# Head 0 loaded straight into its slots, head 1's row maxima placed behind the first scores, and two PSUM banks for turning x where attention ends

## The chip, the cores and the metric

The kernel runs on one core of one Trainium2 chip. The metric is device time of one execution in microseconds (us); less is better. Before the change the median of three runs is 960.9 us (960.69 to 964.77).

## What is computed

Block-sparse attention in float32 over 4 batches of 8 heads, 768 positions and 64 features, then a feed-forward block with a tanh shrink. Cut to what matters:

```python
scores = q @ k.transpose(0, 1, 3, 2) / np.sqrt(64)
mask = window | first and last block | 3 sampled blocks a row   # blocks of 32
scores = np.where(mask, scores, -1e9)
attn = softmax(scores)                  # row maximum subtracted first
x = (attn @ v) -> (3072, 512)
h = x @ w_in                            # 512 x 2048, weights come as int64 words that hold float64
g = h - np.tanh(h)
out = g @ w_out                         # 2048 x 512
```

## The kernel before

**Attention.** Each float32 operand is split into a high part (rounded to the matmul's float32r) and a low part (the rest), and products are made of both. `load_qk` brings the keys and queries of a pair of heads as one `raw` tile of 128 partitions, 64 for each head. `high` (ScalarE, L245) makes `hm`, `low` (GpSimd, L250) makes `lo`, and `dist` (L257) copies the 64 partitions of one head by DMA into that head's slots of one large tile, `slab`: slots A and B (high parts, with the mask rows below them, filled by `fill`, L283) and slots C and D (high and low parts). Head 0's A and B are written by `direct` on VectorE (L253), out of `hm`.

For each head, `smax` (TensorE, L324) makes approximate scores in six tiles of 128 rows, `maxima` (VectorE, L330 for two tiles, L334 for one) takes their row maxima, `turn_max` (TensorE, L337) turns them, `neg_max` (VectorE, L341) negates them, and `put_max` (DMA, L347) writes them as one more row of slot B. Only then can `scores` (TensorE, L356 and L357) make the exact scores with the maximum subtracted inside the product. The work goes in 96 steps, three for each head, and each step has two halves: `scores` into the PSUM tile `pst`, `expo` (ScalarE, L360), `p_high` (ScalarE, L366), `p_low` (GpSimd, L371), and two steps later `accum` (TensorE, L385 to L389) multiplies with v. `smax` has one PSUM tile, `psm`.

**Feed-forward.** Tokens are in six blocks of 512 (n = 0 to 5), the 2048 hidden features in 16 tiles (ft). One unit is one (n, ft): `h_part` (TensorE, L703, 12 matmuls into one of two banks), eleven element operations on ScalarE, VectorE and GpSimd (`g_part`, L713 to L733; VectorE's five are L717, L719, L725, L727 and L729), and `second` (L738 to L740, 12 matmuls into the banks pf0 to pf3). Blocks 0 to 3 are begun during attention with a few ft. Where attention ends, `plan_rest` goes on with the list `SEGS` of (n, first ft, last ft): x=0 is (3, 2, 6), x=1 is (4, 0, 6), x=2 is (5, 0, 16), x=3 is (4, 6, 16). Blocks 4 and 5 must first be turned there: `x_turn` (TensorE, L681, four transposes into bank pf4), `x_high` (ScalarE, L685), `x_low` (VectorE, L689). The weights of ft 6 to 15 are converted there too, 20 of them: three operations on VectorE (L600, L604, L608, through bank pf5 into a buffer `ob`), then ScalarE (L786) and GpSimd (L788). `out_bank` (L797, L799, L801) empties pf0 to pf3 at the end of a segment. For x=1 it writes to the same `ob` buffers, `out_put` (L806) sends them to DRAM, and `get_part` (L758) brings them back into `spare` for x=3.

**The order.** Every step is entered into a `Plan` with a due number, an engine, a duration, and what it reads and writes. `Plan.order` plays the engines against each other and picks on each engine, among the steps that could start within a window `WIN` of the earliest, the one with the smallest due number; the order that comes out is fixed for every engine. DMAs are all issued from SyncE's queue (SP), which is in order too: an issue that waits for a buffer holds up those behind it.

Of the kernel before, what the change touches and what calls it, by code (L numbers as in the profile page):

```python
# [11 lines left out]
F32 = mybir.dt.float32  # L12
# [21 lines left out]
RATE = 1.0  # L34
FT1 = 14
# [9 lines left out]
CHUNK = (28, 52, 68, 84)  # L45

# [24 lines left out]
class Plan:  # L71
# [3 lines left out]
    WIN = {"PE": 0.45, "ACT": 0.3, "DVE": 0.3, "POOL": 0.3, "SP": 0.0}  # L75
# [7 lines left out]
    def order(self):  # L83
# [32 lines left out]
        for _ in range(n):  # L116
            best = None
            for e, c in pools.items():
# [9 lines left out]
                i = min(i for i in c if s[i] <= t0 + self.WIN[e])  # L128
# [87 lines left out]
def attention(ctx, tc, plan, qk, v, samp, blocks, xscr, ident, ffn):  # L216
# [35 lines left out]
    def direct(dst, x):  # L252
        nc.vector.tensor_copy(out=dst[0][0:64], in_=hms[0].bitcast(F32)[0:64, x])  # L253
# [16 lines left out]
    def setup():  # L270
# [6 lines left out]
        nc.vector.tensor_scalar(out=neg[R, :], in0=allow, scalar1=1.0, scalar2=-MASKED, op0=ALU.subtract, op1=ALU.mult)  # L277
        nc.vector.tensor_copy(
# [131 lines left out]
    def at(due, f, *args):  # L410
# [20 lines left out]
        elif n == "direct":  # L431
            eng, dur, r, w, kw = "DVE", dve(768, True), [("hm", 0, args[1])], [("AB"[args[1]], 0)], {"lock": True}
# [6 lines left out]
        elif n == "setup":  # L439
            eng, dur, r, w, kw = "DVE", 1.6, [("st",), ("sp",)], [("mk",)], {"lock": True}  # L440
# [37 lines left out]
        elif n == "p_low":  # L478
            s, x = args
            eng, dur, r, w = "POOL", pool(768), [("pe", s % 2, x), ("ph", s % 3, x)], [("pl", s % 3, x)]  # L480
# [17 lines left out]
    add(-91, "SP", 0.1, lambda: nc.sync.dma_start(out=sp_i[R, :], in_=samp), w=[("sp",)])  # L498
    for x in range(2):
        at(-90 + 0.1 * x, load_qk, 0, x)  # L500
        at(-85 + 0.1 * x, high, 0, x)
        at(-82 + x, direct, (sA, sB)[x], x)
# [4 lines left out]
    at(-86.5, load_qk, 1, slice(0, 2))  # L507
    at(-86, setup)
    at(-84, fill, 0, sA, mk)
    k = -76  # L510
    for c, h in ((CH, 0), (AB, 1), (CL, 0)):
# [18 lines left out]
    k = -63  # L530
# [11 lines left out]
    at(-59, load_v, 0)  # L542
# [16 lines left out]
    for h in range(2, NHEAD):  # L559
# [58 lines left out]
class FFN:  # L618
# [175 lines left out]
    def out_bank(self, x, n, ft, j):  # L794
        nc, o, ob = self.nc, self.banks[j], self.spare[j] if x == 0 else self.ob[j % 2]
# [12 lines left out]
    def turn(self, n, j, x, i):  # L808
        (self.x_turn, self.x_high, self.x_low)[x](n, j, self.xt, *((i,) if x else ()))
# [50 lines left out]
    def unit_ops(self, plan, f, n, ft, h, hq, xi, k, g, gi, halves, **kw):  # L860
# [7 lines left out]
        else:  # L868
            add(f, "PE", 2.72, self.h_part, (n, ft, h, None, xi), rx, [hq], **kw)
# [20 lines left out]
    def plan_rest(self, plan):  # L890
# [104 lines left out]
```

## Time and profile before

| what | value |
|---|---|
| median of 3 runs | 960.9 us |
| the profiled execution's own time | 962.74 us |
| its span, first to last instruction | 961.0 us |
| granted TensorE clock, mean | 0.994 |
| TensorE matmul busy | 903.9 us (94%) |
| VectorE, ScalarE, GpSimd busy | 692.5, 652.3, 531.0 us |
| DMA moved | 123.17 MB |

The span is 1.7 us below the profiled execution's own time, and that execution was 1.8 us above the median. A row of a timeline gives the start and the duration in us, the engine (PE is TensorE, DVE VectorE, ACT ScalarE, POOL GpSimd, SPq the queue that issues DMAs), the source line, what is written and read, and in brackets the idle time ahead of it with what ended it.

### The profile page before, as it was taken

The page shows a single profiled execution, that of the slowest core. Times are in us where ns is not written, and L with a number is a line of the kernel's source. Part 1 is how long each engine was busy: PE and PEld are TensorE (multiplying, and loading weights), DVE is VectorE, ACT ScalarE, POOL GpSimd, SP SyncE. Part 2 cuts the span into 40 slices and gives each one's busy share as a digit, 9 for nine tenths or more (in the row PEclk, how much of TensorE's full clock was granted, in tenths as well). Part 3 has the DMA queues.
Part 4 walks back from the last instruction along what each step waited for, and adds up shares of the span by engine and source line. Part 5 has one row for each costly group of instructions (what it writes and reads, how often), then busy time and mean ns, then how long its engine had stood idle before and what let it go on. Part 6 is the DMA issues. An engine that isn't in the chain of part 4 may idle for free.

```text
span 961.0 us, 18114 instructions
## 1 busy us (share of the span) xinstructions
PE 903.9 (94%) x7072; PEld 748.5 (78%) x7072; DVE 692.5 (72%) x986; ACT 652.3 (68%) x958; POOL 531.0 (55%) x339
## 2 busy tenths in 40 slices
PE   3798889999999999999988999999999999999997
PEld 2586777878888788888867778887888888888885
DVE  4696876779766777777468998966676666766765
ACT  1588878888788888889856666655555555555553
POOL 4479988898888888978863344422222222222221
PEclk9999999999999999999998999999999999999999
DMA  8576666866787566847334253221040310400201
GB/s 223 153 202 181 171 163 192 251 165 182 203 248 192 144 164 184 225 98 218 99 109 145 88 163 102 63 89 45 1 176 1 126 50 6 170 1 0 88 1 44
DMA packets 59052, 123.17 MB, mean 128 GB/s; under 512 B 6336, under 2 KB 27008, under 8 KB 57944
## 3 DMA queue, kind: packets, MB, share of 16 engines
q1 hardware_dynamic: 58968, 122.03, 43.9%
q8 instruction: 55, 0.90, 0.4%
q14 instruction: 29, 0.24, 0.1%
HBM read 56.70 MB, written 27.26 MB: 87 GB/s over the span
## 4 chain that ended last, share of the span: by engine, by line
PE 64%; DVE 22%; ACT 7%; issue 4%; DMA 2%; SPq 0%; DVEq 0%; POOLq 0%; POOL 0%; ACTq 0%
PE bank L703 17%; PE pst L356 7%; PE pst L357 6%; PE psm L324 6%; PE pf L740 4%; PE pf L738 4%; PE pf L739 4%; PE pav L385 3%; PE pav L388 3%; PE pav L389 3%; ACT pe L360 3%; DVE bank L727 2%; DVE t L729 2%; DVE bank L725 2%; DVE t L717 2%
## 5 line engine op out<-in xcount | busy, mean ns | idle before, releaser
L371 POOL TENSOR_TENSOR pl<-pe,ph 128x768 f16<-128x768 f32 x192 | 318.5, 1675 | 79.2 <-ACT ph L366 58.8
L733 POOL TENSOR_TENSOR gl<-t,gh 128x512 fp32r<-128x512 f32 x96 | 123.9, 1291 | 304.6 <-ACT gh L731 250.2
L360 ACT ACTIVATE pe<-pst 128x768 f32<-128x768 f32 x192 | 155.0, 807 | 82.3 <-PE pst L357 81.0
L330 DVE TENSOR_REDUCE mc<-psm 128x2 f32<-128x1536 f32 x90 | 157.8, 1754 | 56.4 <-PE psm L324 56.2
L366 ACT ACTIVATE ph<-pe 128x768 f16<-128x768 f32 x192 | 159.7, 841 | 3.0 <-PE pav L389 0.3
L356 PE MATMUL pst<-slab 128*128 128x512 f32 (+1 forms) x384 | 146.0, 380 | 13.6 <-ACT pe L360 12.9
L723 ACT ACTIVATE u<-u,bias 128x512 f32<-128x512 f32 x96 | 69.5, 724 | 114.8 <-DVE bank L725 114.6
L717 DVE TENSOR_TENSOR t<-t,bank 128x512 f32<-128x512 f32 x96 | 65.7, 684 | 95.3 <-ACT t L715 95.3
L357 PE MATMUL pst<-slab 89*128 89x512 f32 (+1 forms) x384 | 125.6, 347 | 0.0
L385 PE MATMUL pav<-vhl,ph 128*128 128x65 f16 x1152 | 117.9, 194 | 0.1
L388 PE MATMUL pav<-vhl,ph 128*128 128x64 f16 x1152 | 117.0, 195 | 0.0
L389 PE MATMUL pav<-vhl,pl 128*128 128x65 f16 x1152 | 116.4, 193 | 0.0
L385 PEld LDWEIGHTS <-ph 128*128 128x128 f16 x1152 | 106.0, 97 | 8.2 <-issue 5.0
L324 PE MATMUL psm<-slab 88*128 88x512 f32 (+1 forms) x376 | 91.2, 364 | 19.8 <-DMA slab<-hm 12.1
L388 PEld LDWEIGHTS <-ph 128*128 128x128 f16 x1152 | 107.4, 98 | 0.2
L389 PEld LDWEIGHTS <-pl 128*128 128x128 f16 x1152 | 107.3, 99 | 0.0
L731 ACT ACTIVATE gh<-t 128x512 fp32r<-128x512 f32 x96 | 60.5, 630 | 68.8 <-DVE t L729 68.7
L356 PEld LDWEIGHTS pst<-slab 128*128 128x128 f32 x384 | 74.5, 194 | 39.1 <-ACT pe L360 26.7
L738 PE MATMUL pf<-wx,gh 128*128 128x512 f32 x216 | 84.3, 390 | 1.8 <-DVE ob L799 1.7
L740 PE MATMUL pf<-wx,gl 128*128 128x512 f32 x216 | 84.1, 390 | 0.7 <-POOL gl L733 0.7
L324 PEld LDWEIGHTS psm<-slab 88*128 88x128 f32 x376 | 61.5, 201 | 29.6 <-issue 13.0
L739 PE MATMUL pf<-wx,gh 128*128 128x512 f32 x216 | 84.1, 389 | 0.0
(117 smaller groups left out, 1897.3 us busy)
## 6 DMA issues: line engine op xcount, KB each, us to landing
slab<-hm SPq DMA_DIRECT2D x126, 192.0 KB
slab<-lo SPq DMA_DIRECT2D x64, 192.0 KB
raw<-qk SPq DMA_DIRECT2D x15, 768.0 KB
stage<-w_in SPq DMA_DIRECT2D x16, 512.0 KB
stage<-w_out SPq DMA_DIRECT2D x16, 512.0 KB
xsav<-xbuf SPq DMA_DIRECT2D x4, 2048.0 KB
rawv<-v SPq DMA_DIRECT2D x16, 384.0 KB
xscr<-xq SPq DMA_DIRECT2D x16, 384.0 KB
```

The lines of the kernel that those rows point to most:

```text
L324: nc.tensor.matmul(o[:, b0 + c0 : b0 + c1], lhsT=sB[s][0:88, t * P : (t + 1) * P], rhs=sA[s][0:88, c0:c1], start=True, stop=True)
L330: nc.vector.tensor_reduce(out=mcs[h][:, t - 1 : t + 1], in_=psm.rearrange("p (x s) -> p x s", x=2), op=ALU.max, axis=AX.X)
L356: nc.tensor.matmul(pst[:, q], lhsT=sC[c][:, kc], rhs=sD[c][:, q], start=True, stop=False)
L357: nc.tensor.matmul(pst[:, q], lhsT=sA[a][0:89, kc], rhs=sB[a][0:89, q], start=False, stop=True)
L360: nc.scalar.activation(out=pe[s % 2][:, x * S : (x + 1) * S], in_=pst[:, 0:S], func=AF.Exp, scale=0.125)
L366: nc.scalar.activation(out=phs[s][0][:, c], in_=pe[s % 2][:, c], func=AF.Copy)
L371: nc.gpsimd.tensor_tensor(out=pl[:, c], in0=pe[s % 2][:, c], in1=ph[:, c], op=ALU.subtract)
L385: nc.tensor.matmul(oav[:, t, :], lhsT=ph[:, c], rhs=vv[:, 0:65], start=(kt == 0 and t == 0), stop=False, skip_group_check=True)
L388: nc.tensor.matmul(oav[:, t, 0:64], lhsT=ph[:, c], rhs=vv[:, 65:129], start=False, stop=False, skip_group_check=True)
L389: nc.tensor.matmul(oav[:, t, :], lhsT=pl[:, c], rhs=vv[:, 0:65], start=False, stop=last, skip_group_check=True)
L703: self.nc.tensor.matmul(h, lhsT=w[:, cc], rhs=z[:, c, :], start=(c == 0 and x == 0), stop=(c == NCT - 1 and x == 2))
L733: nc.gpsimd.tensor_tensor(out=gl, in0=t, in1=gh.bitcast(F32), op=ALU.subtract)
```

## The change

**At the start.** `load_first` brings raw 0 in two DMAs by head instead of by key and query: 64 partitions with both. `direct` moves to ScalarE and makes head 0's slots A and B out of `raw`, ahead of `high`. `setup` writes the mask also straight into head 0's slot A, and a new `setup_mk` makes the copy for the other heads. Head 0's copies into C and D are ordered ahead of head 1's into A and B; v of pair 0 is loaded much earlier.

**Around the first scores.** Five of head 1's six `smax` tiles get due numbers behind head 0's first scores, all in `psm`; those of heads 2 and 3 are moved by one to two steps. Due numbers of the first weight loads change by half a step.

**Where attention ends.** Turned x of block 4 goes alternately through pf4 and pf5. `h_part` of x=0's ft 4 and 5 is due earlier. The first weight conversion is due three units later (`CONV0`). x=1's result stays in `spare`: the four DMAs out and the four back are gone.

**The planner.** SP's window goes from 0 to 0.25, and to 3.0 for dues below -60. `LOWS` would move some `p_low` to VectorE, but with its values (0, 3) it moves none.

```diff
+CONV0 = 4
+LOWS = (0, 3)
+WSTEP = (2, 5, 8, 11, 14, 17, 20, 23)
-    WIN = {"PE": 0.45, "ACT": 0.3, "DVE": 0.3, "POOL": 0.3, "SP": 0.0}
+    WIN = {"PE": 0.45, "ACT": 0.3, "DVE": 0.3, "POOL": 0.3, "SP": 0.25}
...
-                i = min(i for i in c if s[i] <= t0 + self.WIN[e])
+                win = 3.0 if e == "SP" and ops[min(c)][0] < -60 else self.WIN[e]
+                i = min(i for i in c if s[i] <= t0 + win)
...
+    def load_first(j):
+        if j == 0:
+            raws[0] = p2.tile([P, 2, S], F32, tag="raw", name="raw0", bufs=2)
+        nc.sync.dma_start(out=raws[0][64 * j : 64 * j + 64], in_=qk[0][64 * j : 64 * j + 64])
...
     def direct(dst, x):
-        nc.vector.tensor_copy(out=dst[0][0:64], in_=hms[0].bitcast(F32)[0:64, x])
+        nc.scalar.activation(out=dst[0][0:64], in_=raws[0][0:64, x], func=AF.Copy)
...
+        nc.vector.tensor_copy(
+            out=sA[0][R].rearrange("p (n j) -> p n j", j=BLK), in_=neg[R, :].unsqueeze(2).to_broadcast([NB, NB, BLK])
+        )
+
+    def setup_mk():
...
-            o = ("psm", "pst")[t % 2] if h == 0 or t < 2 else "psm"
-            k = -70 + 8 * h + t if h == 0 or t < 2 else 0.012
+            o = "psm" if h else ("psm", "pst")[t % 2]
+            k = 0.011 + 0.0002 * t if h else -70 + t
...
-    at(-59, load_v, 0)
+    at(-72.5, load_v, 0)
...
+        xs, turn, nmax = (s - 6, s - 5, s - 4), s - 4 + 0.095, s - 3 + 0.012
+        if h < 4:
+            xs, turn, nmax = ((2, 3, 4), 4.095, 5.012) if h == 2 else ((4.015, 5, 5.015), 5.04, 5.041)
...
-        nc, o, ob = self.nc, self.banks[j], self.spare[j] if x == 0 else self.ob[j % 2]
+        nc, o, ob = self.nc, self.banks[j], self.spare[j] if x < 2 else self.ob[j % 2]
...
+        pt = self.cv if n == 4 and j % 2 else self.xt
...
-            add(f, "PE", 2.72, self.h_part, (n, ft, h, None, xi), rx, [hq], **kw)
+            add(first, "PE", 2.72, self.h_part, (n, ft, h, None, xi), rx, [hq], **kw)
...
-            d, i = base + 1 + x / RATE, x % 2
+            d, i = base + CONV0 + x / RATE, x % 2
...
-            if x and f0 and ft == f0 + 3:
+            if x > 3 and ft == f0 + 3:
...
-                    add(d + 0.051 + 0.01 * j, "SP", 0.7, self.out_put, (x, n, ft, j), [ob], w, **late)
+                    if x != 1:
+                        add(d + 0.051 + 0.01 * j, "SP", 0.7, self.out_put, (x, n, ft, j), [ob], w, **late)
```

**SP at the start of the program.** `raw0` is pair 0's keys and queries, `raw1` pair 1's, `rawv0` v of pair 0; the rows that write `slab` from `pe0` and `pe1` are `fill`, from `hm` and `lo` are `dist`, from `nm0` is head 0's `put_max`. Before:

```order
L497 DMA pe0_162<-blocks 24x816
L498 DMA sp_i_159<-samp 24x6
L236 DMA raw0_169<-qk 128x768 x2
L283 DMA slab_78<-pe0_162 24x768
L236 DMA raw1_180<-qk 128x1536
L283 DMA slab_78<-pe0_162 24x768 x2
L283 DMA slab_78<-pe1_163 24x768
L257 DMA slab_78<-hm0_184 64x768 x4
```

And after:

```order
L245 DMA raw0_167<-qk 64x1536
L513 DMA sp_i_159<-samp 24x6
L245 DMA raw0_167<-qk 64x1536
L297 DMA slab_78<-pe0_162 24x768 x2
L249 DMA rawv0_175<-v 128x768
L240 DMA raw1_184<-qk 128x1536
L297 DMA slab_78<-pe0_162 24x768 x2
L266 DMA slab_78<-hm0_189 64x768 x2
L266 DMA slab_78<-lo0_199 64x768 x2
L266 DMA slab_78<-hm0_189 64x768 x2
L297 DMA slab_78<-pe1_163 24x768
L266 DMA slab_78<-hm1_218 64x768
```

The mask row of head 0 (the first row from `pe1` before) no longer goes through the queue, and v comes ahead of pair 1; head 0's `put_max` is the next row of this queue after these, where it was the 27th issue before.

**TensorE around the first scores.** `psm` and `pst` are the two PSUM tiles, L324 (L338 after) is `smax`, L356 and L357 (L370 and L371 after) are `scores`, `mc0` and `mc1` are the maxima of heads 0 and 1, turned. Before:

```order
L324 MATMUL psm_153<-slab_78 128x512
L324 MATMUL psm_153<-slab_78 128x256
L356 MATMUL pst_152<-slab_78 128x512
L357 MATMUL pst_152<-slab_78 128x512
L356 MATMUL pst_152<-slab_78 128x256
L357 MATMUL pst_152<-slab_78 128x256
L337 MATMUL psm_153<-ident_64,mc1_237 6x128
```

And after:

```order
L351 MATMUL psm_153<-ident_64,mc0_192 6x128
L338 MATMUL psm_153<-slab_78 128x512
L338 MATMUL psm_153<-slab_78 128x256
L370 MATMUL pst_152<-slab_78 128x512
L371 MATMUL pst_152<-slab_78 128x512
L370 MATMUL pst_152<-slab_78 128x256
L371 MATMUL pst_152<-slab_78 128x256
```

Before, the first scores stand behind all six tiles of head 1 (the last one is shown), and `turn_max` of head 1 directly behind them; after, one tile of head 1 stands between head 0's `turn_max` and the first scores, and the other five follow one by one between the next scores.

**TensorE where attention ends.** `pf4` and `pf5` are the banks for turned x, `wx32` to `wx35` its tiles, `wo03` and `wo13` (high and low part) go with the rows of `second` for ft 3, the rows into `bank` from `xbuf0` are `h_part` of ft 4 and 5 of x=0. Before, from the second turned tile on:

```order
L681 MATMUL pf4_7274<-ident_64,wx33_7264 128x128 x4
L738 MATMUL pf2_7272<-wo03_141,gh3_94 128x512
L739 MATMUL pf2_7272<-wo13_142,gh3_94 128x512
L740 MATMUL pf2_7272<-wo03_141,gl3_95 128x512
L738 MATMUL pf3_7273<-wo03_141,gh3_94 128x512
L739 MATMUL pf3_7273<-wo13_142,gh3_94 128x512
L740 MATMUL pf3_7273<-wo03_141,gl3_95 128x512
L681 MATMUL pf4_7274<-ident_64,wx34_7265 128x128 x4
L703 MATMUL bank0_76<-xbuf0_81,slab_78 128x512 x12
L681 MATMUL pf4_7274<-ident_64,wx35_7266 128x128 x4
L703 MATMUL bank1_77<-xbuf0_81,slab_78 128x512 x12
```

And after, from the end of ft 2 on:

```order
L760 MATMUL pf3_7273<-wo02_137,gl2_93 128x512
L723 MATMUL bank0_76<-xbuf0_81,slab_78 128x512 x12
L723 MATMUL bank1_77<-xbuf0_81,slab_78 128x512 x12
L701 MATMUL pf4_7274<-ident_64,wx32_7263 128x128 x4
L701 MATMUL pf5_7275<-ident_64,wx33_7264 128x128 x4
L758 MATMUL pf0_7270<-wo03_141,gh3_94 128x512
L759 MATMUL pf0_7270<-wo13_142,gh3_94 128x512
L760 MATMUL pf0_7270<-wo03_141,gl3_95 128x512
L758 MATMUL pf1_7271<-wo03_141,gh3_94 128x512
L759 MATMUL pf1_7271<-wo13_142,gh3_94 128x512
L760 MATMUL pf1_7271<-wo03_141,gl3_95 128x512
L701 MATMUL pf4_7274<-ident_64,wx34_7265 128x128 x4
```

The two `h_part` have moved ahead of all the turns and of ft 3, and the first two turns no longer share a bank. On VectorE four conversions stood before among the turns of block 4; now the first conversion stands behind all of them and the rest follow about one to a unit.

More of the change, by code (lines that the diff above doesn't have):

```diff
@@ L366, in p_high, with low_on_dve @@
         nc.scalar.activation(out=phs[s][0][:, c], in_=pe[s % 2][:, c], func=AF.Copy)
+    def low_on_dve(s, x):
+        return x == 1 and s < LOWS[0] and s % LOWS[1] == 1
     def p_low(s, x):
@@ L479, in at @@
             s, x = args
-            eng, dur, r, w = "POOL", pool(768), [("pe", s % 2, x), ("ph", s % 3, x)], [("pl", s % 3, x)]
+            eng, dur = ("DVE", 0.12 + 1.1e-3 * S) if low_on_dve(s, x) else ("POOL", pool(S))
+            r, w = [("pe", s % 2, x), ("ph", s % 3, x)], [("pl", s % 3, x)]
             kw = {"lock": True}
@@ L497, in attention @@
     add(-92, "SP", 0.1, lambda: nc.sync.dma_start(out=st_sb[R, :], in_=blocks), w=[("st",), ("pe", 0, 0), ("pe", 0, 1)])
-    add(-91, "SP", 0.1, lambda: nc.sync.dma_start(out=sp_i[R, :], in_=samp), w=[("sp",)])
+    add(-91.8, "SP", 0.1, lambda: nc.sync.dma_start(out=sp_i[R, :], in_=samp), w=[("sp",)])
+    for j in range(2):
+        w = [("raw", 0, x, j) for x in range(2)]
+        add(-91.9 + 0.2 * j, "SP", 1.4, load_first, (j,), w=w + ([("raw", 0, 0), ("raw", 0, 1)] if j else []))
     for x in range(2):
-        at(-90 + 0.1 * x, load_qk, 0, x)
-        at(-85 + 0.1 * x, high, 0, x)
-        at(-82 + x, direct, (sA, sB)[x], x)
+        add(-85 + 0.1 * x, "ACT", act(768, False), direct, ((sA, sB)[x], x), [("raw", 0, x, 0)], [("AB"[x], 0)])
+        at(-84 + 0.1 * x, high, 0, x)
         at(-78 + 0.1 * x, low, 0, x)
@@ L506, in attention @@
     at(-87, fill, 0, sB, oh)
-    at(-86.5, load_qk, 1, slice(0, 2))
-    at(-86, setup)
-    at(-84, fill, 0, sA, mk)
+    add(-86, "DVE", 1.9, setup, r=[("st",), ("sp",)], w=[("neg",), ("mA", 0)])
+    add(-85.9, "DVE", 0.6, setup_mk, r=[("neg",)], w=[("mk",)])
+    add(-72, "SP", 3.2, load_qk, (1, slice(0, 2)), [("nm", 0)], [("raw", 1, 0), ("raw", 1, 1)])
     k = -76
-    for c, h in ((CH, 0), (AB, 1), (CL, 0)):
+    for c, h in ((CH, 0), (CL, 0), (AB, 1)):
         for d in c:
@@ L570, in attention @@
                 at(x + 0.02, maxima, h, t)
-        at(s - 4 + 0.095, turn_max, h)
-        at(s - 3 + 0.012, neg_max, h)
-        at(s - 3 + 0.0121, put_max, h)
+        at(turn, turn_max, h)
+        at(nmax, neg_max, h)
+        at(nmax + 0.0001, put_max, h)
     for s in range(NSTEP):
@@ L817, in plan_early @@
             m, ft = "io"[x % 2], x // 2
-            s, i = 2 + 3 * x, x % 2
-            self.stage_op(plan, s - 1.5 if x > 1 else 0.5 + x, m, ft, i)
+            s, i, j = WSTEP[x], x % 2, x % 2
+            self.stage_op(plan, s - 1.5, m, ft, i)
             for n, k in enumerate((0.038, 0.039, 1.038)):
-                add(s + k, "DVE", dve(512), self.convert, (m, ft, n, bank[i]), [("stage", i)], [("bank", i)])
-            add(s + 1.08, "ACT", act(512), self.res_hi, (m, ft, bank[i]), [("bank", i)], [("w", m, 0, ft)])
-            add(s + 2.038, "DVE", dve(512), self.res_lo, (m, ft, bank[i]), [("bank", i), ("w", m, 0, ft)], [("w", m, 1, ft)])
+                add(s + k, "DVE", dve(512), self.convert, (m, ft, n, bank[j]), [("stage", i)], [("bank", j)])
+            add(s + 1.08, "ACT", act(512), self.res_hi, (m, ft, bank[j]), [("bank", j)], [("w", m, 0, ft)])
+            add(s + 2.038, "DVE", dve(512), self.res_lo, (m, ft, bank[j]), [("bank", j), ("w", m, 0, ft)], [("w", m, 1, ft)])
         for x in range(2 * (NPRE - NRES)):
@@ L941, in plan_rest @@
                     e = "DVE" if f0 or j % 2 else "ACT"
-                    ob = ("ob", j % 2) if x else ("spare", j)
+                    ob = ("ob", j % 2) if x > 1 else ("spare", j)
                     r = [("pf", j)] + ([("spare", j)] if f0 else [])
```

26 lines of the change are left out of this document (12 added, 14 removed).

## The prediction

> **What bounds the kernel now.** I read the busy times by stage first, then the timeline of the two stages in which TensorE rests, then the list of its waits. The stages, cut where the work changes (columns: window in us, length, busy us and instructions of each engine, granted clock, DMA share, GB/s):
>
> ```profile
> core 0: us, PE busy (x) PEld busy (x) DVE busy (x) ACT busy (x) POOL busy (x), PEclk, DMA share, GB/s
> 0.00:12.10 12.10, 0.00 (x0) 0.00 (x0) 3.84 (x12) 4.45 (x4) 7.71 (x12) 1.00 0.77 217
> 12.10:25.10 13.00, 9.95 (x25) 6.50 (x26) 7.57 (x9) 0.00 (x0) 3.39 (x1) 1.00 0.93 233
> 25.10:60.80 35.70, 29.77 (x261) 23.87 (x261) 27.64 (x38) 24.05 (x30) 18.22 (x13) 1.00 0.58 159
> 60.80:485.00 424.20, 404.07 (x4677) 340.98 (x4677) 310.92 (x416) 359.03 (x480) 362.20 (x208) 1.00 0.66 181
> 485.00:497.50 12.50, 12.50 (x149) 10.31 (x147) 6.98 (x13) 7.18 (x13) 7.87 (x6) 1.00 0.31 96
> 497.50:518.00 20.50, 14.34 (x57) 10.56 (x56) 16.53 (x26) 9.84 (x17) 7.68 (x7) 0.83 0.63 206
> 518.00:560.00 42.00, 41.31 (x186) 33.75 (x187) 39.98 (x63) 27.52 (x47) 16.70 (x13) 1.00 0.27 88
> 560.00:642.00 82.00, 80.67 (x356) 66.06 (x355) 70.57 (x106) 49.50 (x85) 32.33 (x25) 1.00 0.29 88
> 642.00:961.00 319.00, 311.33 (x1370) 256.51 (x1368) 208.51 (x307) 170.75 (x288) 74.92 (x58) 1.00 0.16 59
> ```
>
> TensorE is the bound nearly throughout: 95 to 98% busy from 60.8 to 485 and from 518 on. It waits at the start, 12.1 us before its first matmul of head 0 and then until 25.1 for the row of maxima, and in 497.5 to 518, where attention ends, with the clock at 0.83. The change touches both.
>
> **The start.** Rows of the timeline (start, duration, engine, line, tiles, idle before):
>
> ```profile
> 1.60 0.83 SPq L236 DMA_DIRECT2D raw<-qk  x2
> 2.93 0.18 DVE L271 CAST sp_f<-sp_i 24x3 f32<-24x3 int32 x1 [1.89 <-DMA sp_i<-samp]
> 4.88 0.84 ACT L245 ACTIVATE hm<-raw 128x768 fp32r<-128x768 f32 x1 [2.86 <-DMA raw<-qk]
> 12.13 0.98 PE L324 MATMUL psm<-slab 88*128 88x512 f32 x2 [12.13 <-DMA slab<-hm]
> 19.23 0.37 PE L337 MATMUL psm<-ident,mc 128*6 128x128 f32 x1 [1.15 <-DVE mc L334]
> 19.98 0.90 SPq L347 DMA_DIRECT2D slab<-nm  x1
> 28.82 0.94 DVE L289 TENSOR_REDUCE am<-rawv 128x1 f32<-128x768 f32 x1
> 25.11 0.63 PE L356 MATMUL pst<-slab 128*128 128x512 f32 x1
> 26.63 0.81 ACT L360 ACTIVATE pe<-pst 128x768 f32<-128x768 f32 x1 [14.68 <-PE pst L357]
> 61.57 0.81 ACT L360 ACTIVATE pe<-pst 128x768 f32<-128x768 f32 x1 [0.39 <-PE pst L357]
> 85.65 0.81 ACT L360 ACTIVATE pe<-pst 128x768 f32<-128x768 f32 x1 [0.40 <-PE pst L357]
> ```
>
> *First approximate scores.* The bytes of raw 0 are the same; the first half, 64 partitions by 6144 bytes (393 KB), is now issued ahead of all else but `blocks`. What queued transfers reach is shown by three stretches of before: halves of raw 0 by key and query, raw 1 with rows of 6144 bytes, and copies of 64 partitions within the core.
>
> ```profile
> 3.50:5.00 1.50, 0.00 (x0) 0.00 (x0) 1.24 (x4) 0.12 (x1) 0.73 (x1) 1.00 1.00 404
> 5.00:7.00 2.00, 0.00 (x0) 0.00 (x0) 0.55 (x1) 1.52 (x2) 1.14 (x1) 1.00 0.96 300
> 8.00:22.00 14.00, 7.24 (x17) 4.18 (x17) 7.62 (x10) 1.48 (x1) 2.34 (x2) 1.00 0.94 214
> ```
>
> No row shows 64 partitions loaded from DRAM. The bounds are 393 KB at 404 and at 214 GB/s, 0.97 and 1.84 us; I take 300, which has the same row length: 1.31. Before, the first half (also 393 KB, at 404) was there at 4.88; issued some 0.4 earlier and 0.34 slower, it is there at 4.8. Two `direct` on ScalarE at 0.84 each (the price of L245, same width) end at 6.5. On VectorE the mask chain took 1.95 us, 2.93 to 4.88; its `samp` is now issued behind that half and lands near 4.7, so the mask is written at about 6.8. The first `smax` starts at 6.9 (6.3 to 7.8), 5.2 ahead of 12.13: the copy `slab<-hm` on which it waited is gone.
>
> [...]
>
> *The row of maxima.* From the first `smax` to the issue of `put_max` it took 19.98 − 12.13 = 7.85 us, bound by TensorE, VectorE and `turn_max` in turn, and that work is the same. v now lands early, so `v_max` (0.94 us) stands ahead of `neg_max` on VectorE; part of it lies in the wait for `turn_max` (1.15 us of such idle time ahead of L337), I add 0.45. Issue: 15.2. But SP's queue has to be through as well: behind raw 0 come v (393 KB at 404), raw 1 (786 KB at 300), four fills of 74 KB and seven copies of 197 KB (1.67 MB at 214): 0.97 + 2.6 + 7.8 = 11.4 us from about 5.8, to 17.2, and some 1.5 until the row itself has landed. First `scores`: 18.9 (17.3 to 20.6) against 25.11, 6.2 earlier. So the transfers end last, not VectorE; moving v earlier costs that 0.97.
>
> *Steps 0 to 6.* Step 6 begins 34.9 us after step 0 (26.63 to 61.57). Undisturbed steps take (85.65 − 61.57) / 6 = 4.01, so 24.1 is the floor and 10.8 is waiting. The floor holds the same work after the change. Now head 1's other five `smax` stand between the scores of head 0, filling TensorE while ScalarE's 0.81 us `expo` run. In exchange head 1's maxima come only just ahead of their use: the row must go VectorE, `turn_max`, VectorE, DMA, and its `put_max` stands in SP behind a copy that waits for a slot. By the same chain of head 0 (from `turn_max` at 19.23 to 25.11, 5.9 us, some of it covered by two steps of head 0) I allow 3.5; for the first `accum`, whose v is converted on VectorE between the maxima, 2; for the row of head 2, which comes a step nearer to its use, 2.1. That is 7.6, less than the 10.8 of before since head 1's tiles now fill gaps. Step 6: 18.9 + 1.5 (25.11 to 26.63) + 24.1 + 7.6 = 52.1 against 61.57, **9.5** earlier. Bounds: 5, if the row of head 2 costs 3.5 as well and `accum` 5; 13.5, if about half of the 7.6 comes.
>
> From step 7 on the order on TensorE is nearly as before, and its waits there are for ScalarE, which keeps its place:
>
> ```profile
> PEld pst L356 <- ACT pe L360: 24.5, 43, 1.2
> ```
>
> (us, number, longest, from 60 to 485; no transfer is in the list for these.) So the gain goes through the middle unchanged, and SP's window of 0.25 and `LOWS` cost nothing: the cover is the two steps by which rows come ahead of their scores.
>
> **Where attention ends.** Rows on TensorE and VectorE:
>
> ```profile
> 499.45 0.63 PE L681 MATMUL pf<-ident,wx 128*128 128x128 f32 x4 [1.79 <-DMA wx<-xscr]
> 505.20 1.12 PE L681 MATMUL pf<-ident,wx 128*128 128x128 f32 x4 [0.82 <-DVE slab L689]
> 509.37 3.03 PE L703 MATMUL bank<-xbuf,slab 128*128 128x512 f32 x12
> 514.33 0.68 DVE L717 TENSOR_TENSOR t<-t,bank 128x512 f32<-128x512 f32 x1
> 518.03 2.34 PE L703 MATMUL bank<-slab,wi 128*128 128x512 f32 x9 [1.99 <-DVE t L729]
> 499.60 0.72 DVE L729 COPY_PREDICATED t<-u,bank 128x512 f32<-128x512 int32 x1
> 585.72 0.70 DVE L600 TENSOR_SCALAR pf<-stage 128x512 int32<-128x512 int32 x1
> 587.86 0.68 DVE L717 TENSOR_TENSOR t<-t,bank 128x512 f32<-128x512 f32 x1
> 591.41 0.70 DVE L600 TENSOR_SCALAR pf<-stage 128x512 int32<-128x512 int32 x1
> 558.71 1.52 PE L703 MATMUL bank<-xbuf,wi 128*128 128x512 f32 x6
> 625.85 2.93 PE L703 MATMUL bank<-xbuf,wx 128*128 128x512 f32 x12
> 932.53 2.88 PE L703 MATMUL bank<-slab,wx 128*128 128x512 f32 x12
> 937.97 2.88 PE L703 MATMUL bank<-slab,wx 128*128 128x512 f32 x12
> ```
>
> A unit takes (937.97 − 932.53) = 5.44 on TensorE, so an `h_part` or a `second` 2.72. In the 20.5 us from 497.5 stand two `h_part`, one `second` and five turns of about 0.4: 10.2 us of work, 10.3 lost. Each turn waited for the one bank pf4 to be read by `x_low` (505.20), and block 4's first `h_part` at 518.03 for VectorE's L729.
>
> After: the two `h_part` run from 497.5 and from 500.3 (when L729 at 499.60 frees the bank), 5.5 us that cover the loads on which 499.45 waited. VectorE's first operation of ft 4 comes 1.9 us after its `h_part` (512.4 to 514.33), at 502.2. From there VectorE sets the end: five operations of ft 4, four `x_low`, one of ft 5, ten at 0.69, and 0.9 of waits on ScalarE: 510.0 for block 4's first `h_part`, 8.0 ahead.
>
> *What is given back.* Four conversions stood in the hole; they come later, among the units. One is 587.86 − 585.72 = 2.14 us on VectorE, a unit with one 591.41 − 585.72 = 5.69, so without one 3.55: slightly over TensorE's 5.44, so while conversions last VectorE sets the pace. From the end of the first `h_part` (512.8) to ft 1 of x=2 stand six units, five conversions and eight single operations: 21.3 + 10.7 + 5.5 = 37.5, so 550.3 against 558.71. Then twelve units at 5.69 and two single operations of `out_bank`, 0.65 each: 69.6, so ft 13 at 619.9 against 625.85, **6.0** earlier. The conversions are over about there, and TensorE leads again. The last weight is ready three units (16.3 us) later; before it had 18.2 us in hand, so nothing waits, with 1.9 to spare. x=1's eight DMAs no longer exist; they lay beside other work, 0. Bounds: 9 if VectorE's waits (11.4 us idle of 82 in 560 to 642) take in the conversions; 2 if each conversion also delays a TensorE unit by its misfit.
>
> **Sum.** 9.5 + 6.0 = 15.5. The profiled execution took 962.74 for its span of 961.0, that is 947.2 after; against the median of 960.9, **945.4**. From about 956.1 to 965.7 (0.5%) a measurement could hardly tell it from no change.
>
> **The rivals.** *A, both parts carry* (0.55): 945.4. *B, the conversions swallow the gain of the transition* (0.18): VectorE is busy 39.98 of 42 us in 518 to 560, so moving 8.6 us of conversions there returns all; against it stand the 11.4 us idle in the next stage. 960.9 − 9.5 = 951.4. *C, half of the start's waits do not come, and the transition keeps its whole 9* (0.11): 960.9 − 13.5 − 9 = 938.4. *D, the transfers hold head 0's row* (0.05): DMA is at 0.94 in 8 to 22, and fewer than seven copies fit ahead; scores 3 earlier, 952. *E, slower* (0.05): SP's window of 0.25 puts each head's `put_max` behind one more 197 KB copy, 197 / 214 = 0.92 us; if that landing is what the head's scores wait for, 30 heads times 0.92 is 27.6: 945.4 + 27.6 = 973.0. It decides as soon as the rows have under 0.92 us in hand; against it no wait of TensorE for a transfer is in the middle's list. *F, nothing carries* (0.06): the start's gain is waited away by step 12, where heads 2 and 3 have no rows, and B holds; about 960.
>
> **How the numbers follow.** The forecast is A's, the likeliest. A's own bounds are 960.9 − 5 − 2 = 953.9 and 960.9 − 13.5 − 9 = 938.4; B, C and D lie within them, E and F, 0.11 together, outside, and each of B to D spreads by some 2 around its price. That makes 936 to 955. Faster by over 0.5%: A to D, 0.89; within: F, 0.06; slower: E, 0.05.
>
> **What would show it.** Right: the first `smax` near 6.9, the first scores near 18.9 behind a transfer, step 6 at 52, `h_part` of block 4 some 8 us closer to the end of attention with the clock at 1.00 there, and ft 13 of x=2 about 15.5 earlier than 625.85. Wrong: first half of raw 0 later than 5.5 (the split is slow); steps of over 4.1 us in the middle with waits for transfers (E); VectorE without idle time between 520 and 600 and TensorE waiting for L729 at each unit (B); a first `scores` after 21 (D).

## The result, and the profile after

The changed kernel takes 956.2 us (median of 8, 952.9 to 957.4) against 960.54 before (median of 8 beside it): ratio 0.9946, interval 0.9924 to 0.9968. It is faster by 0.54%, about 5 us, a third of the 15.5 forecast, and just above the range (936 to 955). The profiled execution took 957.11 us with a span of 955.3.

The stages of the profile after, cut as before the change (columns: window, length, busy us and instructions by engine, granted clock, DMA share, GB/s):

```profile
core 0: us, PE busy (x) PEld busy (x) DVE busy (x) ACT busy (x) POOL busy (x), PEclk, DMA share, GB/s
8.40:21.50 13.10, 6.46 (x15) 3.76 (x16) 6.61 (x8) 2.38 (x3) 3.59 (x2) 1.00 0.88 222
21.50:61.00 39.50, 35.33 (x283) 27.68 (x282) 26.57 (x36) 24.34 (x31) 23.08 (x13) 1.00 0.72 178
61.00:88.60 27.60, 23.88 (x257) 19.84 (x254) 22.84 (x33) 22.01 (x28) 20.29 (x12) 0.88 0.72 200
88.60:485.00 396.40, 381.15 (x4418) 323.09 (x4417) 286.62 (x388) 337.00 (x453) 340.46 (x196) 1.00 0.65 180
497.20:510.00 12.80, 11.94 (x60) 9.27 (x58) 9.04 (x15) 8.42 (x15) 3.92 (x4) 1.00 0.45 149
510.00:560.00 50.00, 49.09 (x221) 39.29 (x219) 47.14 (x73) 31.43 (x54) 19.41 (x15) 1.00 0.31 96
```

The hole of 20.5 us where attention ended (14.34 busy, clock 0.83) is now 12.8 with 11.94 busy and the clock at 1.00. But attention ends at 497.2, where it ended at 497.5: in these two profiles nothing of the start's lead is left there. One profile does not settle that, though: the same mark stands at 492.8 in a second profile of the changed kernel (after_again below) and at 493.7 with the start as before (turn_only below). Three rows of the timeline answer to the rows at 518.03, 558.71 and 625.85 of before (a row counts only the matmuls inside the window that was asked for, hence x9, x10 and x6 for an `h_part` of 12):

```profile
509.96 2.27 PE L723 MATMUL bank<-slab,wi 128*128 128x512 f32 x9
549.68 2.55 PE L723 MATMUL bank<-xbuf,wi 128*128 128x512 f32 x10
618.53 1.66 PE L723 MATMUL bank<-xbuf,wx 128*128 128x512 f32 x6
```

They stand 8.1, 9.0 and 7.3 us earlier, where 8.0, 8.4 and 6.0 were forecast. The rows of the start:

```profile
5.60 1.57 ACT L262 ACTIVATE slab<-raw 64x768 fp32r<-64x768 f32 x2 [3.58 <-DMA raw<-qk]
8.38 0.98 PE L338 MATMUL psm<-slab 88*128 88x512 f32 x2 [8.38 <-DMA slab<-pe]
16.92 0.74 SPq L361 DMA_DIRECT2D slab<-nm  x1
20.76 0.98 PE L338 MATMUL psm<-slab 88*128 88x512 f32 x2 [4.90 <-DMA slab<-pe]
21.53 0.63 PE L370 MATMUL pst<-slab 128*128 128x512 f32 x1
23.05 0.81 ACT L374 ACTIVATE pe<-pst 128x768 f32<-128x768 f32 x1 [6.72 <-PE pst L371]
60.98 0.81 ACT L374 ACTIVATE pe<-pst 128x768 f32<-128x768 f32 x1 [0.24 <-PE pst L371]
88.56 0.80 ACT L374 ACTIVATE pe<-pst 128x768 f32<-128x768 f32 x1
```

The first half of raw 0 is there at 5.60 (4.8 forecast), the first smax runs at 8.38 (6.9), `put_max` is issued at 16.92 (15.2), and the first scores start at 21.53 (18.9), behind head 1's tile, which waited 4.9 us for its mask row. The lead is 3.6 us there, 0.6 at step 6 (60.98 against 61.57) and −2.9 at step 12 (88.56 against 85.65). In after_again, the same program, the first scores start at 18.96 and step 12 at 83.65, leads of 6.2 and 2.0. So how large the lead is at first differs between profiles; that 4 to 6.5 us of it are lost by step 12 does not.

One thing in these rows is not in the column of the granted clock. The starts of consecutive matmuls of 512 columns show TensorE's rate (the matmul of the first row of each pair has 512):

```profile
42.52 0.63 PE L370 MATMUL pst<-slab 128*128 128x512 f32 x1
42.95 0.63 PE L371 MATMUL pst<-slab 89*128 89x512 f32 x1
...
48.02 0.39 PE L371 MATMUL pst<-slab 89*128 89x512 f32 x1
48.25 0.28 PE L370 MATMUL pst<-slab 128*128 128x256 f32 x1
```

Until 47.6 they start 0.43 us apart, from then on 0.23; I call these half rate and full rate. Before the change it was the same until 48.6, and the column says 1.00 in both. The rate changes within the first `accum`.

### The profile page after: what moved, and what is told of

It is laid out like the page before. It is cut to its first block, busy times and chain, and to the rows that moved or that the text cites. A ratio compares the mean times of both kernels' runs of the same rounds, so it can differ in the third digit from the quotient of the medians.

```text
span 955.3 us, 18092 instructions
## 1 busy us (share of the span) xinstructions
PE 905.9 (95%) x7072; PEld 748.7 (78%) x7072; DVE 687.2 (72%) x985; ACT 653.4 (68%) x960; POOL 530.5 (56%) x339
## 4 chain that ended last, share of the span: by engine, by line
PE 63%; DVE 22%; ACT 7%; issue 3%; DMA 3%; POOL 1%; SPq 1%; DVEq 0%; POOLq 0%; ACTq 0%
PE bank L723 17%; PE pst L370 8%; PE pst L371 6%; PE psm L338 5%; PE pf L760 4%; PE pf L758 4%; PE pf L759 4%; ACT pe L374 3%; PE pav L403 3%; PE pav L406 3%; PE pav L407 3%; DVE t L749 3%; DVE bank L745 3%; DVE bank L747 3%; DVE t L737 2%
## 5 line engine op out<-in xcount | busy, mean ns | idle before, releaser
L370 PE MATMUL pst<-slab 128*128 128x512 f32 (+1 forms) x384 | 146.8, 382 | 14.5 <-ACT pe L374 13.7
L743 ACT ACTIVATE u<-u,bias 128x512 f32<-128x512 f32 x96 | 69.5, 724 | 114.6 <-DVE bank L745 114.3
L371 PE MATMUL pst<-slab 89*128 89x512 f32 (+1 forms) x384 | 126.9, 350 | 0.1
L403 PE MATMUL pav<-vhl,ph 128*128 128x65 f16 x1152 | 120.0, 196 | 0.0
L406 PE MATMUL pav<-vhl,ph 128*128 128x64 f16 x1152 | 119.1, 197 | 0.0
L407 PE MATMUL pav<-vhl,pl 128*128 128x65 f16 x1152 | 118.5, 194 | 0.0
L403 PEld LDWEIGHTS <-ph 128*128 128x128 f16 x1152 | 107.2, 98 | 8.2 <-issue 5.0
L338 PE MATMUL psm<-slab 88*128 88x512 f32 (+1 forms) x378 | 91.7, 363 | 19.0 <-DMA slab<-pe 13.3
L406 PEld LDWEIGHTS <-ph 128*128 128x128 f16 x1152 | 108.7, 99 | 0.1
L370 PEld LDWEIGHTS pst<-slab 128*128 128x128 f32 x384 | 75.1, 196 | 41.1 <-ACT pe L374 29.1
L371 PEld LDWEIGHTS pst<-slab 89*128 89x128 f32 x384 | 75.9, 198 | 12.0 <-DMA slab<-nm 0.5
```

What stands on the lines that cost most here:

```text
L338: nc.tensor.matmul(o[:, b0 + c0 : b0 + c1], lhsT=sB[s][0:88, t * P : (t + 1) * P], rhs=sA[s][0:88, c0:c1], start=True, stop=True)
L370: nc.tensor.matmul(pst[:, q], lhsT=sC[c][:, kc], rhs=sD[c][:, q], start=True, stop=False)
L371: nc.tensor.matmul(pst[:, q], lhsT=sA[a][0:89, kc], rhs=sB[a][0:89, q], start=False, stop=True)
L403: nc.tensor.matmul(oav[:, t, :], lhsT=ph[:, c], rhs=vv[:, 0:65], start=(kt == 0 and t == 0), stop=False, skip_group_check=True)
L406: nc.tensor.matmul(oav[:, t, 0:64], lhsT=ph[:, c], rhs=vv[:, 65:129], start=False, stop=False, skip_group_check=True)
L407: nc.tensor.matmul(oav[:, t, :], lhsT=pl[:, c], rhs=vv[:, 0:65], start=False, stop=last, skip_group_check=True)
```

## The experiments

Where each stands in attention, read from the first `expo` of a step in its timeline (us), and its median time with the ratio to before, which ran beside it on the same chip:

| kernel | step 0 | step 6 | step 18 | step 30 | time | ratio, interval |
|---|---|---|---|---|---|---|
| before | 26.6 | 61.6 | 111.0 | 165.6 | 960.2 to 961.5 | |
| after | 23.1 | 61.0 | 113.2 | 165.7 | 956.2 | 0.9946 (0.9924 to 0.9968) |
| after_again | 20.5 | 57.2 | 108.3 | 159.8 | 955.1 | 0.9936 (0.9913 to 0.9958) |
| start_only | 21.1 | 58.2 | 110.1 | 162.6 | 963.1 | 1.0027 (1.0014 to 1.0039) |
| turn_only | 24.9 | 61.0 | 110.4 | 161.8 | 954.5 | 0.9942 (0.9921 to 0.9963) |
| scores_first | 21.1 | 59.5 | 110.7 | 162.3 | 956.0 | 0.9953 (0.9935 to 0.9970) |
| by_key | 20.1 | 57.5 | 109.9 | 162.4 | 954.2 | 0.9934 (0.9915 to 0.9954) |
| max_back | 24.7 | 57.8 | 108.1 | 161.8 | 952.9 | 0.9934 (0.9915 to 0.9952) |
| busy_pe | 22.8 | 59.9 | 111.6 | 164.2 | 955.8 | 0.9956 (0.9939 to 0.9972) |
| busy_rows | 20.9 | 55.9 | 108.5 | 160.1 | 951.6 | 0.9907 (0.9889 to 0.9926) |
| key_busy | 20.0 | 54.9 | 106.8 | 159.4 | 950.7 | 0.9893 (0.9871 to 0.9914) |
| busy_hm88 | 23.9 | 60.7 | 112.4 | 164.9 | 956.4 (one run) | |
| hold | 22.4 | 60.0 | 111.8 | 163.4 | 954.9 | 0.9936 (0.9918 to 0.9953) |
| busy_all | 21.0 | 55.4 | 106.8 | 158.5 | 957.5 | 0.9965 (0.9945 to 0.9985) |
| key_busy_all | 18.8 | 53.2 | 104.6 | 157.5 | 956.2 | 0.9953 (0.9934 to 0.9971) |
| conv_first | 22.3 | 59.7 | 112.2 | 164.7 | 960.5 | 0.9992 (0.9976 to 1.0008) |
| one_bank | 22.0 | 59.6 | 112.1 | 164.7 | 958.7 | 0.9972 (0.9952 to 0.9992) |
| turn_busy | 31.8 | 63.0 | 112.4 | 163.9 | 959.9 | 0.9976 (0.9957 to 0.9996) |

Profiles of one start differ by 0.6 to 5.9 us in these columns (after and after_again are the same program, and before and turn_only have the same start), so a single column of a single profile proves little. Lengths of steps repeat better.

### Which half carries the gain

start_only: the edits at the end of attention undone. turn_only: these alone, put into the kernel before.

> The changed kernel with its end of attention as before (turns through one bank, conversions from the first unit on, x=1 by way of DRAM); the start stays changed. Theory 1, the lead of the start is eaten before step 30 (3.6 us at the first scores, 0.6 at step 6, none at step 30, as in the profile after): 960.5, within 2 us of before, ratio 1.000. Rival, the start is worth its lead and the profile after fell on a run with a bad clock: 957 or less. As predicted on record (start alone 9.5): 951.

> The kernel before with the changed end of attention alone. Theory 1: the whole gain is here, 5 to 6 us, 955, the same as the changed kernel. Rival, the gain of the changed kernel is shared by both parts: 957 to 959. First h_part of block 4 some 8 us nearer to the end of attention in either case.

turn_only has the whole gain; the changed start alone has none, and is even 0.27% slower. Its attention ended about 3 us earlier than before in the profile; behind it, twelve matmuls of block 4's first `h_part` took 4.51 us against 3.0, in part at half rate again. The granted clock of its twelve executions is 0.989 to 0.992, that of the 17 of before beside them 0.991 to 0.996, so the other executions probably had more half rate too; why it comes there stays open. The 9.5 forecast for the start are refuted.

### The order of the first scores, and the same program again

```diff
# behind Plan.order
+ tile = [smax(1, 0), maxima(1, 0)]
+ # moved to the place behind scores(0, 0)
```

> The changed kernel with one exchange: head 1's first tile of smax stands behind head 0's first scores instead of ahead. In the profile after, that tile waited for the mask row of head 1 (DMA, 4.9 us of idle time) at 20.76 with the scores behind it. If head 0's row of maxima had landed by then, the first scores come 1 to 2 us earlier, near 19.5; if the row itself is late, they stay at 21.5. The total: theory 1 says no change whatever the scores do (956); the rival that leads carry says 1 to 2 less.

> The changed kernel again, beside the next three on one chip. All theories: 956, 0.994 to 0.996 of before. If its half-speed stretch at 67 to 75 us belongs to the changed start it is there again; if it was an accident of one execution it is gone and step 12 comes at 86 instead of 88.6.

scores_first takes 956.0, and its first `expo` at 21.1 lies between those of after (23.1) and after_again (20.5), so what it does to the first scores is undecided. In after_again the half-rate stretch was there (66.3 to 69.4). It stands in every profile with the changed start, unless the maxima are moved back or matmuls are added there, and in none with the start as before: it belongs to the changed start. That step 12 comes at 83.6 all the same shows how far one profile carries.

### How raw 0 is loaded

```diff
-out=raws[0][64 * j : 64 * j + 64], in_=qk[0][64 * j : 64 * j + 64]
+out=raws[0][:, j], in_=qk[0][:, j]
```

> The changed kernel with raw 0 in two loads of 128 partitions, keys and then queries, instead of two of 64 partitions by head; the rest in the same order. In the profile after, each half of 64 partitions took some 2 us to land (5.60 and 7.72 are the first uses). Theory, 64 partitions load at half rate: both loads of 128 are there by about 6, the first smax at about 7.8 instead of 8.4, the first scores up to 1 earlier. Rival, both forms load at one rate: the first direct only starts when its key half lands, the second one later: first smax at 8.4 or later. Total 956 in both, since leads of the start are lost by step 12.

```profile
4.87 0.84 ACT L262 ACTIVATE slab<-raw 64x768 fp32r<-64x768 f32 x1 [2.84 <-DMA raw<-qk]
6.22 0.84 ACT L262 ACTIVATE slab<-raw 64x768 fp32r<-64x768 f32 x1 [0.51 <-DMA raw<-qk]
```

Each row waits for one load of 393 KB. The second is there 1.35 us behind the first, 291 GB/s; in the profile after, the second half by head was first used at 7.72, 2.1 behind 5.60, 186 GB/s. So in these two profiles 64 partitions load at under two thirds of the rate, and the forecast's 300 GB/s was wrong for them. The rate for 128 partitions does not repeat: in key_busy and key_busy_all, which load the same way, the second half is there 2.69 and 2.19 behind the first, 146 and 180 GB/s. What does repeat is when both halves are there: by 5.9 to 7.1 in the six profiles that load 128 partitions, by 7.6 to 8.4 in the twelve that load 64. The first smax came at 7.12 in by_key; the time changed by less than the intervals tell apart.

### Half rate at the start

busy_pe, busy_hm88 and busy_rows add the same 14 matmuls where TensorE stood idle, three ahead of head 0's `turn_max` and eleven behind it; they differ in the operands. busy_pe and busy_hm88 use 88 rows of the array, busy_rows 128.

```diff
# cut to the matmuls; the lines that place them are left out
+ for n in (512, 512, 256) + (512,) * 11:
+     matmul(ffn.hb[1][:, 0:n], lhsT=sB[0][0:88, 0:P], rhs=sA[0][0:88, 0:n])    # busy_pe
+     matmul(ffn.hb[1][:, 0:n], lhsT=hms[0][:, 1, 0:P], rhs=hms[0][:, 0, 0:n])  # busy_rows; [0:88, ...]: busy_hm88
```

> The changed kernel with 14 idle-time matmuls more (head 0's operands into a bank that nobody reads): three ahead of turn_max of head 0, eleven behind it, where TensorE stood idle for 1.15 and 4.9 us. In both kernels matmuls of 512 columns start 0.43 us apart until the first long stretch without a gap (47.6 us after, 48.6 before) and 0.23 apart from then on, while the column of the granted clock says 1.00 throughout. Theory 1a, half speed until that stretch is what ate the lead: with TensorE kept busy from 12.5 on the full rate comes near 20, half steps of 2.55 become 2.0, step 6 at about 56 instead of 61, and if leads carry 952 in all. Theory 1b, something else sets the middle (copies, GpSimd, weights): step 6 at 56 but step 30 unchanged at 165.6, and 956. Rival, TensorE's rate has another cause: 0.43 until 47 all the same, step 6 at 61, 956.

> As the run with 14 more matmuls at the start, which filled 7.5 us without a gap and left TensorE at 0.43 us per 512 columns until 46; but these 14 use all 128 rows of the array (pair 0's rounded keys and queries) instead of 88. [...]

> The kernel with 14 matmuls at the start, of the same operands as the one that reached full rate at 18 us, but 88 rows of them instead of 128. If the rows in use decide: 0.43 us per 512 columns until the first accumulations (44 to 47). If it was the data: full rate at 18 us.

The eleven matmuls of busy_pe, of busy_rows with the scores behind them, and of busy_hm88:

```profile
15.39 5.04 PE L547 MATMUL bank<-slab 88*128 88x512 f32 x11
21.32 0.63 PE L370 MATMUL pst<-slab 128*128 128x512 f32 x1
21.75 0.63 PE L371 MATMUL pst<-slab 89*128 89x512 f32 x1
```

```profile
15.89 3.87 PE L547 MATMUL bank<-hm 128*128 128x512 f32 x11
19.96 0.40 PE L370 MATMUL pst<-slab 128*128 128x512 f32 x1
20.19 0.40 PE L371 MATMUL pst<-slab 89*128 89x512 f32 x1
```

```profile
15.80 5.04 PE L547 MATMUL bank<-hm 88*128 88x512 f32 x11
```

With 88 rows TensorE worked from 12.9 to 20.4 with one pause of 0.08 us and stayed at 0.43 until 46 (busy_hm88 until 46.6, with the same data as busy_rows); with 128 rows it came to 0.23 near 18. So the rows in use decide here, not only being busy, and the data is not it. Long matmuls of 128 rows alone are not needed, though: in max_back (below) the rate rose near 34.3, seven us ahead of its first `accum`, in 3.6 us without a pause of `scores` (128 and 89 rows in turn) and `smax` (88). Where the bound lies is not shown.

At full rate the first four half steps took 7.55 us instead of 10.25. But TensorE fell back to half rate from 32.0 to 42.1, and step 6 came 35.1 us behind step 0, where the changed kernel takes 36.7 and 37.9. The time fell to 951.6 (950.0 to 952.7), 3.5 less than the changed kernel beside it (after_again, 951.7 to 956.0); the intervals of the two ratios still overlap. With raw 0 loaded by keys and queries as well it is 950.7, the lowest median here, 1.07% under before; but the first smax came at 8.00 there, not at the 7.1 expected, so this does not show whether a lead at that point carries.

> The 14 matmuls of 128 rows at the start together with raw 0 in two loads of 128 partitions (first smax at 7.1 us instead of 8.4 there). If a lead at the first smax carries: 1.3 less than 951.6, 950. If the row of maxima or the queue ends last as before: first scores no earlier than 19.5, 951.6.

### Steps 6 to 12

hold adds 20 matmuls into unused columns of `pst`:

```diff
+ # behind scores(7, 0): 8 times, behind scores(7, 1): 12 times
+ matmul(pst[:, 768:1024], lhsT=ffn.wi[0][0][:, 0:P], rhs=ffn.wi[0][0][:, 0:256])
```

> The changed kernel with 20 matmuls more in steps 6 to 8, 128 rows by 256 columns of a weight into columns of pst that nobody reads: eight behind the first half of step 7's scores and twelve behind the second, where TensorE waited 1.0 us for VectorE's maxima and 1.5 us for ScalarE. In every kernel with the changed start TensorE falls to half rate for 3 to 5 us right behind these two waits (67 to 75), and steps 6 to 12 take 26.4 to 27.9 us, against 24.0 with the start as before, where it does not. Theory A, the fall of the rate is what these steps lose: no half-rate stretch at 67 to 75, steps 6 to 12 in 25 us, total 1.5 to 2.5 less than after, 953 to 954. Theory B, the two waits themselves are the loss: steps 6 to 12 in 27 as before, total 955 to 956.

```profile
60.00:87.20 27.20, 24.37 (x277) 20.00 (x274) 23.27 (x33) 22.05 (x29) 20.52 (x12) 1.00 0.76 205
```

The clock is 1.00, where it was 0.88 after, and the six steps still take 27.2 us (27.6 after). That looks like theory B, but the extra matmuls were in the way themselves: they write into `pst`, and the `expo` behind the first eight waited for them.

```profile
65.46 0.81 ACT L383 ACTIVATE pe<-pst 128x768 f32<-128x768 f32 x1 [1.50 <-PE pst L370]
```

The first three half steps from step 6 on took 8.8 us, against 7.1 after and 5.8 before; the next four, at full rate, 8.4, against 10.5 after (9.5 in after_again) and 7.9 before. So both theories have a part: in the profile after, the waits cost these steps 1.3 us and the half-rate stretch behind them 2.7 (1.6 in after_again), and later half steps give 0.5 back; hold removed the second and lengthened the first. The same six steps of turn_only, with the start as before:

```profile
61.00:85.00 24.00, 21.48 (x256) 17.26 (x255) 18.86 (x24) 20.28 (x25) 21.09 (x13) 1.00 0.82 206
```

VectorE has 23.27 us of work there with the changed start and 18.86 without. Eight operations of the weight conversion stand in these steps instead of four, two more that make low parts of weights, one more that makes the low part of v. About half of them were put off from steps 0 to 6, which have three more operations for the maxima and two conversions, one low part and one operation on v fewer; the others stood in steps 12 to 18 before. So part of the lead at step 6 was work not yet done.

busy_all and key_busy_all extend busy_rows and key_busy by 49 matmuls like those of hold: in the waits of steps 0 to 3 (24), behind accum(4) (8), and as in hold (5 and 12).

> The kernel with 14 matmuls of 128 rows at the start (951.6 us; full rate from 18 us, lost again at 32 to 42, 56 to 59 and 66 to 69) with 49 more of 128 rows by 256 columns in the waits ahead of those three falls. Theory A: full rate from 18 us on throughout, step 6 at 53 and step 12 at 78, against 55.9 and 83.9, and 946 to 948 in all. Theory B, the waits are the loss and the extra matmuls only fill them: full rate but steps as long as before, 951 to 952.

> All three together: the two loads of 128 partitions, the 14 matmuls at the start, the 49 in later waits. Theory A: 945 to 948. Theory B: 950 to 952.

Full rate lasted from 18 to 199 us in busy_all, yet step 6 came at 55.4 (busy_rows 55.9), step 18 at 106.8 (108.5), and the time rose to 957.5. Both theories' totals fail. It is no clean trial of full rate either: the extra matmuls read `hm`, and the `high` that overwrites it waited for them, so that step 3 came 8.8 us behind step 2 (7.3 after):

```profile
35.58 1.49 ACT L254 ACTIVATE hm<-raw 128x1536 fp32r<-128x1536 f32 x1 [3.12 <-PE pst L370]
```

Against busy_rows the profile has new half-rate stretches at 199.6 and 649; the second of them stands in after_again too, without extra matmuls. The ten executions of busy_all go from 953.45 us at a granted clock of 0.997 to 961.48 at 0.988, and the profiled one, 954.03 at 0.995, is among the shortest, so the others probably had more half rate than the profile shows. What brings it is open.

max_back undoes the moved maxima alone:

```diff
-            o = "psm" if h else ("psm", "pst")[t % 2]
-            k = 0.011 + 0.0002 * t if h else -70 + t
+            o = ("psm", "pst")[t % 2] if h == 0 or t < 2 else "psm"
+            k = -70 + 8 * h + t if h == 0 or t < 2 else 0.012
...
-        if h < 4:
-            xs, turn, nmax = ((2, 3, 4), 4.095, 5.012) if h == 2 else ((4.015, 5, 5.015), 5.04, 5.041)
```

> The changed kernel with the row maxima of heads 1 to 3 due as before the change (four tiles of head 1 ahead of the first scores); loads, direct copies and end of attention as changed. With the change, steps 0 to 18 take 87 to 90 us against 85.5 with the start as before, and that eats a lead of 4 at the first scores. Theory, the maxima put behind the scores are what makes those steps longer, since VectorE's work for them is the same and only moves: first scores 2 to 3 later than after, steps 0 to 18 in 85 to 87, total 953 to 956. Rival, the maxima were well moved and the early loads make the steps longer: total 958 or more.

Steps 0 to 18 take 83.4 us, against 90.1 after, 87.8 in after_again and 84.4 before: the moved maxima made them longer. Steps 6 to 12 take 24.4 us here, with 20.15 us of work on VectorE and without the half-rate stretch. 952.9 in all is not told apart from after by the intervals, but moving the maxima gained nothing.

> The end of attention as changed, the start as before, and 26 matmuls of 128 rows by 256 columns in TensorE's waits between 15 and 29 us. Theory, rows in use open the clock: full rate from about 27 instead of 49, steps 0 to 6 in 32 to 33 us instead of 36.1, total 951 to 952, as good as with the changed start and its 14 matmuls. Rival, the start as before waits for VectorE and transfers rather than TensorE: full rate, but steps 0 to 6 in 36, total 954.5.

turn_busy puts 128-row matmuls of 256 columns into the kernel with the start as before: 5 ahead of head 0's `turn_max`, 6 ahead of smax(1, 2), 12 behind scores(0, 0), 3 behind head 1's `turn_max`. It is a miss of placement: its 26 matmuls stood in the way, and the first `expo` came at 31.8. Steps 0 to 6 then took 31.2 us instead of 36.1, but TensorE was at full rate only from 27 to 38.6, and with the first `expo` 7 us later other work may have been done by then, so this does not show what full rate is worth.

### Where attention ends

```diff
-CONV0 = 4
+CONV0 = 1                                             # conv_first
...
-        pt = self.cv if n == 4 and j % 2 else self.xt
+        pt = self.xt                                  # one_bank, with the planner's resource likewise
```

> The changed kernel with the first weight conversion due three units earlier, as before the change; on VectorE one conversion then stands ahead of the turns of block 4 and two between them and ft 5. Theory 1 (the working on record: VectorE sets the pace from the end of attention to the last conversion, so a conversion costs 2.14 wherever it stands): first h_part of block 4 some 4 later than after, ft 13 of x=2 level with it within 1, total 956 to 957. Rival, conversions hide in VectorE's idle time later on and cost only in the hole: total 959 to 960.

> The changed kernel with the turns of block 4 through one bank, as before. The planner then puts four conversions among those turns again, as before the change, though the first is due three units later. Theory, a conversion in the hole costs its 2.14 us of VectorE and one among the units about 0.25 (5.69 against 5.44), which is what the run with conversions three units earlier showed: total 959 to 961, no gain left. Rival, the early h_part and x=1 kept in SBUF carry the gain: 956 to 957.

conv_first loses the whole gain (960.5): the rival. Its ft 13 of x=2, counted from the end of attention (the first `h_part` behind it, 497.2 after and 496.3 here), stands at 128.0 against 121.3:

```profile
624.34 1.90 PE L723 MATMUL bank<-xbuf,wx 128*128 128x512 f32 x7
```

Three conversions, 6.4 us of VectorE, stand in the hole, and ft 13 is 6.7 later; the end of the program is 5.1 later (463.2 from the same mark, against 458.1). So the three units at the end that then have no conversion give back only 1.6, since a unit with one takes 5.69 on VectorE and one without still 5.44 on TensorE. My expectation took VectorE for the pace of every unit alike. one_bank puts four conversions back and takes 958.7, so by the medians the second bank brings about half the gain, by letting the turns go ahead of them; its interval overlaps with that of after. What keeps the other half there, the early `h_part` or x=1 left in `spare`, was not tested alone.

## Why the prediction was right or wrong

- **Where attention ends: right**, in sum (6.0; 5.7 in the spans, 5.5 to 6 in turn_only) and at its waypoints: block 4's first `h_part` at 510.0 forecast, 509.96 measured; x=2's ft 1 550.3 and 549.68; ft 13 619.9 and 618.53.
- **First approximate scores and the row: mis-sized.** The halves of 64 partitions loaded at 186 GB/s in the profile after, not at 300, so 1.5 of the forecast 5.2 were missing at the first smax (8.3 to 8.9 in the profiles that load so). The scores gained 3.6 instead of 6.2; ahead of them stood head 1's tile, waiting for a mask row behind the copies, which the working didn't price. In after_again that wait was 2.3 us instead of 4.9 and the scores came at 18.96, as forecast; by step 12 it had lost 4 us of that lead all the same, so the larger error lies behind the first scores.
- **"Steps 0 to 6": failed.** The floor of 24.1 us was six steps at 4.01, taken from steps 6 to 12, which run at full rate. Until the first `accum` TensorE runs at half: 23.05 to 35.9 is five half steps of 2.57, where 2.0 was counted. That is 2.9 of the 6.2 us by which steps 0 to 6 ran over (37.9; 31.7 forecast). The other 3.3 lie in the half steps behind them, four of which took 3.5 to 5.1 us; how they divide between half rate, which lasts until 47.6, and waits for which 7.6 was too little, stays open. Starting earlier only starts earlier at half rate, since in both kernels the rate rises within the first accumulations (47.6 us after, 48.6 before). The 10.8 us read as waiting before the change were in part the same half rate: the prediction's table has TensorE busy for 29.77 of 35.70 us there, so it can have waited for 5.9 at most. The column of the granted clock showed 1.00 and I did not look at the spacing of the matmuls; the row at 25.11 of before (0.63 for 512 columns, against 0.39 later) showed it. busy_rows confirms the term: five half steps of 1.9 at the start, and 3.5 us less in all.
- **"The gain goes through the middle unchanged": failed from step 6 to step 12.** They took 27.6 instead of 24.1 (26.5 in after_again). VectorE's work was put off into them; the waits it brought cost 1.3, and the fall to half rate behind them 1.6 to 2.7. With the maxima back neither is there (max_back, 24.4). From step 12 to the last step it does hold: 393.6 us after, 394.1 in after_again, 393.6 in turn_only with the start as before (396.8 in before's own profile, with a half-rate stretch at 137.7). Rival F had this loss by step 12, at 0.06; the outcome itself, a start worth nothing beside an end of attention that carries, was not among the rivals.
- So of 9.5 for the start nothing arrives; that is nearly the whole error. On top of the floor I had allowed for waits only (7.6), not for another rate. That the end of attention alone comes out as forecast rests on turn_only, not on the profiles' equal ends of attention, which were chance.

## What to carry to other kernels

Price a stage with durations from that stage: a pace read a few steps later can belong to another rate, here 0.23 us per 512 columns on TensorE instead of 0.43. Check TensorE's rate by the spacing of equal matmuls, not by a clock column (at the start it said 1.00 at both), and ask which work ran just before the rate changed. And a lead at one step counts only if the same work has been done by then: compare the operations of each engine between two marks, not the marks alone. Where a trial adds work to fill waits, look in its trace for who waits for the added work before reading its time.

## What the runs showed of the hardware

- TensorE stayed at half rate through 7.5 us of matmuls with 88 rows and one pause of 0.08 us (busy_pe; busy_hm88 likewise), and came to full rate within 4 us of such with 128 rows (busy_rows); half rate is 0.43 us from one matmul of 512 columns to the next, full rate 0.23. A mixture of 128, 89 and 88 rows did reach full rate once, in max_back at 34.3.
- It fell back to half rate for stretches of 2.5 to 5 us, and of 10 in busy_rows (32.0 to 42.1), behind waits of 0.4 to 2.7 us: in after behind 1.0 and 1.5 (69.5 to 74.8), in busy_rows behind five of 0.4 to 0.6. Where these stretches lie late in the program differed between the two profiles of the changed kernel: 122.8 in after, 315 and 650 in after_again.
- Loads of 393 KB, from the arrivals of two in a row: 186 GB/s into 64 partitions (after), 291 GB/s into 128 (by_key; 146 in key_busy).
